# The second chunk's packed weights one step later, and the weight conversion as one stream through the second batch's attention

## The chip, the cores and the metric

The kernel runs on one core of a Trainium2 chip. The metric is device time in microseconds (us). Before the change the median of 3 runs is 812.47 us, from 811.91 to 814.41.

## The reference, cut to what matters

```
p_packed = sm_attn(p, k, v)             # 8 batches, 8 heads: 32 packed queries, 576 keys
out = sm_attn(q, p_packed, p_packed)    # 576 queries against the 32 packed rows
x = out.transpose(0, 2, 1, 3).reshape(B * S, H * D)     # 4608 tokens x 512
h = x @ w_in                            # 512 x 2048
g = h * tanh(softplus(h))               # "Mish"
return g @ w_out                        # 2048 x 512
```

Here `sm_attn(q, k, v)` is softmax(q k^T / 8) v. The two weight matrices come in as 64-bit floating-point numbers and are turned into 32-bit ones on the chip.

## The kernel before, in words

**Work per batch.** A batch's attention ends in a matrix `aT` (second softmax, transposed), held as a high and a low part, `aT_hi` and `aT_lo`. The values of the second attention are folded into `w_in`: `packed_w(b, c)` (L421) multiplies the packed rows of batch b with 512 columns of `w_in` (a *chunk* c, four of them) and splits the result into `wp_hi` (ScalarE, L439) and `wp_lo` (VectorE, L440). Then the work goes in *steps* t (`step`, L597), one for each pair of batch and 128 columns of `w_in`: `up` (L479) makes two halves of h with 6 matmuls each, ScalarE applies Mish (L482, L484), `halves` splits g into `g_hi` (ScalarE cast, L491, in the steps below 16) and `g_lo` (VectorE, L492), and two steps later `down` (L496 to L498) multiplies g with the matching 128 rows of `w_out` into four accumulators. So step t on TensorE is: a quarter of the down of step t-2, up half 0, two quarters of down, up half 1, the last quarter.

**Order of the steps.** `TURNS` lets batch 0 (`first`) do its columns 0 to 7 in steps 0 to 7, then batch 1 (`second`) all its 16 columns in steps 8 to 23, then batch 0 the rest. A chunk's packed weights are made at the end of the step named in L635: before the change, of every step with t % 4 == 2, so chunk 1 of batch 0, first read in step 4, is made at the end of step 2; chunk 0 of batch 1 at the end of step 6.

**Weight conversion.** Of each weight tile (`Weight` for 128 rows and 1024 columns of `w_in`, `WeightOut` for 128 rows of `w_out`) `fetch` issues a 512 KB load on the sync queue, `words` (L378, L379) is two ScalarE instructions, `join` (L383, L386, L387, L390) four VectorE instructions, and `done` either stores a pair of `w_in` tiles to DRAM (L395) or splits a `w_out` tile: `hi` is a ScalarE cast (L411) and `lo` a VectorE subtraction (L412). The list `weights` fixes their order: tiles 0 to 3 are the first half of `w_in`, tile 4 is `w_out` 0, then the second half's four tiles that chunk 1 needs (`w_in` chunk pair c = 1: tiles 5 to 8), then `w_out` 1 to 7 as tiles 9 to 15. The generator `conversion(n)` (L577) runs through them: an odd call does join(n), an even one words(n+1) and done(n). `take` calls it so many times; `step` takes half of its `n_conv` calls between the two up halves' places and the rest behind them.

**Who orders what.** TensorE's order is the order of the code throughout. Up to step 15 VectorE, ScalarE and the sync queue are in the order of the code too (`manual_schedule`); behind that a scheduler places them. Each engine works its list strictly in this order, so an instruction that waits holds up all that stands behind it.

**The start.** Lines L651 to L748 write out the attention of the first two batches by hand, with the conversions of tiles 0 to 5 between its pieces. `second.score_now(0)` (L706) is the first matmul of the second batch's keys; `exps_now` are its two exponentials on ScalarE; `first.weigh` finishes batch 0's second softmax on VectorE (L309 to L312), transposes it (L317), lets ScalarE cast it to `aT_hi` (L318) and subtracts to `aT_lo` (L319). `second.turn`, `turn_weights`, `values`, `turn_values` and `match` are batch 1's further pieces, `second.peak` and `second.weigh` its second softmax. Steps 0 and 1 stand between these pieces; steps 2 and on stand behind all of them, with 3 calls of the conversion in each of steps 2 to 7.

Of the kernel before, what the change touches and what calls it, by code (L numbers as in the profile page):

```python
# [8 lines left out]
F32 = mybir.dt.float32  # L9
# [26 lines left out]
def body(  # L36
# [101 lines left out]
    class Batch:  # L138
# [166 lines left out]
        def weigh(self, gs):  # L305
            a2 = self.a2[:, gs].rearrange("a h g n -> a (h g) n")
            G = a2.shape[1]
            sm = stat.tile([P, 2 * (S // NP)], F32, name="sm2")[:, :G]
            nc.vector.reduce_sum(out=sm, in_=a2, axis=AX.X)  # L309
            nc.vector.tensor_scalar(out=sm, in0=sm, scalar1=1e-9, scalar2=None, op0=ALU.add)  # L310
            nc.vector.reciprocal(out=sm, in_=sm)
            nc.vector.tensor_tensor(  # L312
                out=a2, in0=a2, in1=sm.unsqueeze(2).to_broadcast([P, G, NP]), op=ALU.mult
            )
            for g in range(gs.start, gs.stop):
                at = att.tile([P, S], F32, name="at", bufs=1)
                nc.vector.transpose(out=at, in_=self.a2[:, g].rearrange("a g n -> a (g n)"))  # L317
                nc.scalar.copy(out=self.aT_hi[:, g, :], in_=at)  # L318
                nc.vector.tensor_tensor(  # L319
                    out=self.aT_lo[:, g, :], in0=at, in1=self.aT_hi[:, g, :].bitcast(F32), op=ALU.subtract  # L320
                )

        def attention(self):


            self.start(ps_a)
            yield
            for g in range(2):
                yield from self.score(g, ps_a)
            self.exps(slice(0, 2))  # L330
            for g in range(2):
                yield from self.turn(g, ps_a)
            self.sums()
            for g in range(2):
                yield from self.turn_weights(g, ps_a)
                yield from self.values(g, ps_a)
            for g in range(2):
                yield from self.turn_values(g, ps_a)
            for g in range(2):
                yield from self.match(g, ps_a)  # L340
            self.peak(slice(0, 2))
            yield
            self.weigh(slice(0, 2))

    class Weight:

# [223 lines left out]
            paired[b // 2 * 2, f // 4] = t  # L570
    paired = {t: x for x, t in paired.items()}

    weights = [Weight(0, m) for m in range(4)] + [WeightOut(0)] + [Weight(1, m) for m in range(4)]
    weights += [WeightOut(i) for i in range(1, 8)] + [Weight(2, m) for m in range(4)] + [WeightOut(8)]
    weights += [Weight(3, m) for m in range(4)] + [WeightOut(i) for i in range(9, NF)]

    def conversion(n):  # L577
# [19 lines left out]
    def step(t, n_att, n_conv, cast):  # L597


        nonlocal gen  # L600
        grp = None
        if t < len(order):
            b, f, begin, end = order[t]
            if t == 20:
                gen = batches[2].attention()
            if b > 1 and f == 0 and b + 1 < B:
                gen = batches[b + 1].attention()
            if b > 1 and f == 10 and b + 2 < B:
                batches[b + 2].load()
            grp = Group(b, f, begin, end, wps[b, f // 4], g_rests[b // 2])  # L610
            grp.tiles()
        groups.append(grp)
        dn = groups[t - LAG] if t >= LAG else None
        if dn:
            down(dn, 0)
        if grp:
            grp.up(0)
        take(conv, n_conv // 2)
        take(gen, n_att[0])
        if dn:  # L620
            down(dn, 1)
            down(dn, 2)
        take(gen, n_att[1])
        if grp:
            grp.up(1)
        take(conv, n_conv - n_conv // 2)
        if grp:
            grp.halves(cast)
        if t - 1 in paired:
            pb, i = paired[t - 1]  # L630
            rest["g"] = split(g_rests[pb // 2][0, i], g_rests[pb // 2][1, i])
        if dn:
            down(dn, 3)
        n = t // 4 + 1
        if t % 4 == 2 and n < len(chunks):  # L635
            nb, nch = chunks[n]
            if nch == 0:
                together(gen)
            wps[nb, nch] = packed_w(nb, nch)
            if n >= 7 and n + 1 < len(chunks):  # L640
                fetch_wi(chunks[n + 1][1])
        else:
            take(gen, n_att[2])
        if t - 2 in paired:
            down_rest(*paired[t - 2])

    gen = iter(())
    with tc.manual_schedule(engines={mybir.EngineType.PE}):
# [4 lines left out]
        with tc.manual_schedule(engines={mybir.EngineType.DVE, mybir.EngineType.Activation, mybir.EngineType.SP}):  # L653
            for g in range(2):
                first.load_k(g)
                if g == 0:
                    first.load_p()
            w[0].fetch()
            for g in range(2):
                first.load_q(g)  # L660
            w[1].fetch()
            first.start(ps_a)
            first.turn_keys(0)
            first.score_now(0)
            w[0].words()
            sums = [first.exps_now(0)]
            first.turn_keys(1)
            for g in range(2):
                first.load_v(g)
            w[2].fetch()  # L670
            w[3].fetch()
            w[0].join()
            first.score_now(1)
            w[1].words()
            sums.append(first.exps_now(1))
            together(first.turn(0, ps_acc))
            w[1].join()
            w[1].done()
            first.sums_now(0, sums[0])
            together(first.turn_weights(0, ps_acc))  # L680
            together(first.turn(1, ps_acc))
            first.sums_now(1, sums[1])
            second.load_k(0)
            second.load_p()
            second.load_k(1)
            w[4].fetch()
            together(first.values(0, ps_a))
            together(first.turn_weights(1, ps_acc))
            w[2].words()
            w[2].join()  # L690
            together(first.values(1, ps_a))
            for g in range(2):
                together(first.turn_values(g, ps_a))
            w[3].words()
            for g in range(2):
                together(first.match(g, ps_acc))
            for g in range(2):
                second.load_q(g)
            w[5].fetch()
            for g in range(2):  # L700
                first.peak(slice(g, g + 1))
            second.start(ps_a)
            second.turn_keys(0)
            w[3].join()
            w[3].done()
            second.score_now(0)  # L706
            first.weigh(slice(0, 1))
            sums = [second.exps_now(0)]
            second.turn_keys(1)
            for g in range(2):  # L710
                second.load_v(g)
            for n in range(6, 11):
                w[n].fetch()
            wps = {(0, 0): packed_w(0, 0)}
            second.score_now(1)
            first.weigh(slice(1, 2))
            sums.append(second.exps_now(1))
            groups = []
            g_rests = [{} for _ in range(B // 2)]
            conv = iter(())  # L720
            together(second.turn(0, ps_acc))
            second.sums_now(0, sums[0])
            together(second.turn_weights(0, ps_acc))
            step(0, (0, 0, 0), 0, nc.scalar.copy)
            together(second.turn(1, ps_acc))
            second.sums_now(1, sums[1])
            w[4].words()
            w[4].join()
            together(second.values(0, ps_a))
            together(second.turn_weights(1, ps_acc))  # L730
            w[5].words()
            w[4].done()
            conv = conversion(5)
            together(second.values(1, ps_a))
            step(1, (0, 0, 0), 2, nc.scalar.copy)
            for g in range(2):
                together(second.turn_values(g, ps_a))
            for g in range(2):
                together(second.match(g, ps_acc))
            for g in range(2):  # L740
                second.peak(slice(g, g + 1))
            take(conv, 2)
            second.weigh(slice(0, 1))
            take(conv, 2)
            second.weigh(slice(1, 2))
            take(conv, 2)
            for t in range(2, START):
                step(t, (0, 0, 0), 3 if t < 8 or t == 11 else 1 if t == 10 else 2, nc.scalar.copy)  # L748
        for t in range(START, len(order) + LAG):
            if t in (16, 26):  # L750
                batches[t // 10 + 1].load()
# [27 lines left out]
```

## Time and profile before

| | |
|---|---|
| median of 3 runs | 812.47 us (811.91 to 814.41) |
| the profiled execution | 809.08 us |
| its span, first to last instruction | 807.3 us |
| TensorE matmul busy | 765.5 us, 95% of the span |
| VectorE busy | 441.9 us, 55% |
| ScalarE busy | 323.2 us, 40% |
| DMA mean rate | 106 GB/s |
| chain that ended last, by engine | PE 88%, DVE 9%, ACT 2% |

In the rows PE is TensorE's matmuls, PEld its weight loads, DVE is VectorE, ACT ScalarE, SPq the sync queue. A timeline row gives start, duration, engine, line, operation, the tile written and the tiles read, and in square brackets how long the engine sat idle before it and whose end released it. The durations of PE rows overlap, since matmuls are pipelined: the distance from one start to the next is the cost of one. PEclk is the share of full speed that TensorE's clock had.

### The profile page before, as it was taken

The page shows a single profiled execution, that of the slowest core. Times are in us where ns is not written, and L with a number is a line of the kernel's source. Part 1 is how long each engine was busy: PE and PEld are TensorE (multiplying, and loading weights), DVE is VectorE, ACT ScalarE, POOL GpSimd, SP SyncE. Part 2 cuts the span into 40 slices and gives each one's busy share as a digit, 9 for nine tenths or more (in the row PEclk, how much of TensorE's full clock was granted, in tenths as well). Part 3 has the DMA queues.
Part 4 walks back from the last instruction along what each step waited for, and adds up shares of the span by engine and source line. Part 5 has one row for each costly group of instructions (what it writes and reads, how often), then busy time and mean ns, then how long its engine had stood idle before and what let it go on. Part 6 is the DMA issues. An engine that isn't in the chain of part 4 may idle for free.

```text
span 807.3 us, 13715 instructions
## 1 busy us (share of the span) xinstructions
PE 765.5 (95%) x5584; PEld 608.5 (75%) x5584; DVE 441.9 (55%) x846; ACT 323.2 (40%) x752; POOL 0.7 (0%) x6
## 2 busy tenths in 40 slices
PE   7565799999999999999999999999999999999997
PEld 6344477887878787878788787888788787878886
DVE  4867887695457537354563546445473445532332
ACT  4353667563433424234342443334242343332221
POOL 0000000000000000000000000000000000000000
PEclk9667699999999999999999999999999999999999
DMA  9993205532522541242311532144311411131002
GB/s 251 302 293 113 104 27 157 161 127 79 172 90 79 158 141 59 76 138 92 111 53 59 176 96 76 56 154 125 112 53 53 137 40 54 53 105 53 1 1 65
DMA packets 42814, 85.82 MB, mean 106 GB/s; under 512 B 8448, under 2 KB 26880, under 8 KB 42752
## 3 DMA queue, kind: packets, MB, share of 16 engines
q1 hardware_dynamic: 42752, 84.95, 34.5%
q8 instruction: 44, 0.72, 0.4%
q14 instruction: 18, 0.15, 0.1%
HBM read 71.30 MB, written 13.63 MB: 105 GB/s over the span
## 4 chain that ended last, share of the span: by engine, by line
PE 88%; DVE 9%; ACT 2%; issue 1%; DMA 0%; SPq 0%; DVEq 0%; ACTq 0%
PE ps_h L479 25%; PE acc L496 15%; PE acc L498 14%; PE acc L497 14%; PE ps_w L428 4%; PE ps_kq L120 4%; PE ps_s L129 3%; PE ps_rest L496 2%; PE ps_rest L498 2%; PE ps_rest L497 2%; PE ps_pp L260 1%; PE ps_a L251 1%; DVE wi L387 1%; DVE wo L387 1%; DVE wo L390 1%
## 5 line engine op out<-in xcount | busy, mean ns | idle before, releaser
L496 PE MATMUL acc<-wo,g_hi 128*128 128x512 f32 x512 | 214.4, 419 | 1.9 <-ACT wo L411 1.1
L482 ACT ACTIVATE g<-ps_h 128x288 f32<-128x288 f32 (+1 forms) x256 | 98.2, 385 | 279.7 <-PE ps_h L479 229.2
L498 PE MATMUL acc<-wo,g_lo 128*128 128x512 f32 x512 | 202.6, 396 | 1.9 <-DVE g_lo L492 1.9
L497 PE MATMUL acc<-wo,g_hi 128*128 128x512 f32 x512 | 202.5, 395 | 0.0
L479 PE MATMUL ps_h<-aT_hi,wp_hi 128*128 128x288 f32 x512 | 157.6, 308 | 0.0
L491 DVE CAST g_hi<-g 128x512 fp32r<-128x512 f32 x112 | 47.8, 426 | 196.6 <-ACT g L482 196.6
L479 PE MATMUL ps_h<-aT_hi,wp_lo 128*128 128x288 f32 x512 | 152.8, 298 | 0.0
L479 PE MATMUL ps_h<-aT_lo,wp_hi 128*128 128x288 f32 x512 | 152.6, 298 | 0.0
L496 PEld LDWEIGHTS acc<-wo,g_hi 128*128 128x128 f32 x512 | 96.7, 189 | 45.1 <-issue 23.9
L498 PEld LDWEIGHTS acc<-wo,g_lo 128*128 128x128 f32 x512 | 96.8, 189 | 25.4 <-DVE g_lo L492 3.1
L479 PEld LDWEIGHTS ps_h<-aT_hi,wp_hi 128*128 128x128 f32 x512 | 97.6, 191 | 14.8 <-issue 5.6
L479 PEld LDWEIGHTS ps_h<-aT_lo,wp_hi 128*128 128x128 f32 x512 | 97.8, 191 | 8.8
L497 PEld LDWEIGHTS acc<-wo,g_hi 128*128 128x128 f32 x512 | 97.2, 190 | 8.6 <-DVE wo L412 0.4
L492 DVE TENSOR_TENSOR g_lo<-g,g_hi 128x512 fp32r<-128x512 f32 x128 | 88.2, 689 | 18.0 <-ACT g_hi L491 12.4
L479 PEld LDWEIGHTS ps_h<-aT_hi,wp_lo 128*128 128x128 f32 x512 | 97.7, 191 | 0.2 <-DVE wp_lo L440 0.2
L428 PE MATMUL ps_w<-wi,ppT 64*32 64x512 f32 x512 | 40.0, 628 | 13.7 <-DVE wi L390 10.1
L440 DVE TENSOR_TENSOR wp_lo<-ps_w,wp_hi 128x512 fp32r<-128x512 f32 x64 | 41.2, 682 | 19.1 <-ACT wp_hi L439 19.1
L439 ACT CAST wp_hi<-ps_w 128x512 fp32r<-128x512 f32 x64 | 34.4, 591 | 30.4 <-PE ps_w L428 30.4
L120 PEld LDWEIGHTS ps_kq<-ident,k_t 96*128 96x128 f32 x192 | 23.3, 162 | 6.8 <-issue 4.4
L484 ACT ACTIVATE g_rest<-ps_h 128x64 f32<-128x64 f32 x128 | 28.1, 219 | 0.0
L428 PEld LDWEIGHTS ps_w<-wi,ppT 64*32 64x32 f32 x512 | 6.4, 106 | 28.2 <-DVE wi L390 12.7
L120 PEld LDWEIGHTS ps_kq<-ident,q_t 96*128 96x128 f32 x192 | 21.9, 152 | 6.9 <-issue 3.0
(91 smaller groups left out, 753.4 us busy)
## 6 DMA issues: line engine op xcount, KB each, us to landing
wi<-w_in_f SPq DMA_DIRECT2D x48, 512.0 KB, 4.5
k_t<-in_k_dram SPq DMA_DIRECT2D x32, 288.0 KB, 3.6
q_t<-in_q_dram SPq DMA_DIRECT2D x32, 288.0 KB, 4.0
v_t<-in_v_dram SPq DMA_DIRECT2D x32, 288.0 KB, 3.9
w_st<-in_moe_w_in_dram SPq DMA_DIRECT2D x16, 512.0 KB, 6.4
w_st<-in_moe_w_out_dram SPq DMA_DIRECT2D x16, 512.0 KB, 4.4
out_dram<-o SPq DMA_DIRECT2D x24, 192.0 KB, 2.5
w_in_f<-wi SPq DMA_DIRECT2D x8, 512.0 KB, 4.8
```

The source lines that it names most:

```text
L120: nc.tensor.transpose(out=ps[:, h, :], in_=of_slot(src, g, h)[:, i, :], identity=ident[:R, :R])
L428: nc.tensor.matmul(out=ps[g][h * NP:(h + 1) * NP, :], lhsT=ppTb[row:row + D, g, h * NP:(h + 1) * NP], rhs=wis[c, g][row:row + D, h // 2, : ...
L439: nc.scalar.copy(out=hi, in_=ps[g])
L440: nc.vector.tensor_tensor(out=lo, in0=ps[g], in1=hi.bitcast(F32), op=ALU.subtract)
L479: nc.tensor.matmul(out=ps, lhsT=w[:, fs], rhs=a[:, g, cs], start=(n == 0), stop=(n == 5))
L482: nc.scalar.activation(out=self.act[:, hf * HALF:hf * HALF + m], in_=ps[:, :m], func=AF.Mish)
L484: nc.scalar.activation(out=self.g_rest[self.b % 2, self.f // 4][:, self.f % 4, :], in_=ps[:, m:], func=AF.Mish)
L491: cast(out=hi, in_=self.act)
L492: nc.vector.tensor_tensor(out=lo, in0=self.act, in1=hi.bitcast(F32), op=ALU.subtract)
L496: nc.tensor.matmul(out=acc, lhsT=hi[:, cs], rhs=wh, start=start, stop=False)
L497: nc.tensor.matmul(out=acc, lhsT=hi[:, cs], rhs=wl, start=False, stop=False)
L498: nc.tensor.matmul(out=acc, lhsT=lo[:, cs], rhs=wh, start=False, stop=stop)
```

## The change

Five edits, all in the part before step 16.

1. `weigh` is cut in three: `weigh` (the softmax's end), `back` (transpose and the ScalarE cast to `aT_hi`) and `low` (the subtraction to `aT_lo`), so that other work can stand between them.
2. `w_out` 1 becomes tile 5 of the list, ahead of the second half of `w_in`, whose four tiles become 6 to 9. `w_out` 2 to 7 stay tiles 10 to 15.
3. The conversion becomes one stream from tile 4 on: words(4) right behind `packed_w(0, 0)`, then a call or two behind nearly every piece of the second batch's attention and in steps 0 to 3. Steps 4 to 7 take 3, 2, 1 and 3 calls.
4. Chunk 1 of batch 0 is packed at the end of step 3 instead of step 2.
5. `first.weigh` moves behind the second batch's exponentials and key transposes; the second batch's scores for its second half stand ahead of `packed_w(0, 0)`; steps 2 and 3 now stand ahead of `second.weigh` of the first and of the second half.

```diff
@@ Batch.weigh
-            for g in range(gs.start, gs.stop):
-                at = att.tile([P, S], F32, name="at", bufs=1)
-                nc.vector.transpose(out=at, in_=self.a2[:, g].rearrange("a g n -> a (g n)"))
-                nc.scalar.copy(out=self.aT_hi[:, g, :], in_=at)
-                nc.vector.tensor_tensor(
-                    out=self.aT_lo[:, g, :], in0=at, in1=self.aT_hi[:, g, :].bitcast(F32), op=ALU.subtract
-                )
+        def back(self, g):
+            self.at = att.tile([P, S], F32, name="at", bufs=1)
+            nc.vector.transpose(out=self.at, in_=self.a2[:, g].rearrange("a g n -> a (g n)"))
+            nc.scalar.copy(out=self.aT_hi[:, g, :], in_=self.at)
+
+        def low(self, g):
+            nc.vector.tensor_tensor(
+                out=self.aT_lo[:, g, :], in0=self.at, in1=self.aT_hi[:, g, :].bitcast(F32), op=ALU.subtract
+            )
...
-    weights = [Weight(0, m) for m in range(4)] + [WeightOut(0)] + [Weight(1, m) for m in range(4)]
-    weights += [WeightOut(i) for i in range(1, 8)] + [Weight(2, m) for m in range(4)] + [WeightOut(8)]
+    weights = [Weight(0, m) for m in range(4)] + [WeightOut(0), WeightOut(1)]
+    weights += [Weight(1, m) for m in range(4)] + [WeightOut(i) for i in range(2, 8)]
+    weights += [Weight(2, m) for m in range(4)] + [WeightOut(8)]
...
-        if t % 4 == 2 and n < len(chunks):
+        if t % 4 == (2 if t > 3 else 3) and n < len(chunks):
...
             second.score_now(0)
-            first.weigh(slice(0, 1))
             sums = [second.exps_now(0)]
             second.turn_keys(1)
...
+            first.weigh(slice(0, 1))
+            first.back(0)
+            second.score_now(1)
+            first.low(0)
+            sums.append(second.exps_now(1))
+            first.weigh(slice(1, 2))
+            first.back(1)
             wps = {(0, 0): packed_w(0, 0)}
-            second.score_now(1)
-            first.weigh(slice(1, 2))
-            sums.append(second.exps_now(1))
+            w[4].words()
+            first.low(1)
...
-            conv = iter(())
+            conv = conversion(4)
             together(second.turn(0, ps_acc))
             second.sums_now(0, sums[0])
             together(second.turn_weights(0, ps_acc))
-            step(0, (0, 0, 0), 0, nc.scalar.copy)
+            take(conv, 1)
+            step(0, (0, 0, 0), 2, nc.scalar.copy)
             together(second.turn(1, ps_acc))
             second.sums_now(1, sums[1])
-            w[4].words()
-            w[4].join()
             together(second.values(0, ps_a))
             together(second.turn_weights(1, ps_acc))
-            w[5].words()
-            w[4].done()
-            conv = conversion(5)
+            take(conv, 2)
             together(second.values(1, ps_a))
             step(1, (0, 0, 0), 2, nc.scalar.copy)
...
             take(conv, 2)
+            step(2, (0, 0, 0), 2, nc.scalar.copy)
             second.weigh(slice(0, 1))
-            take(conv, 2)
+            second.back(0)
+            take(conv, 1)
+            second.low(0)
+            take(conv, 1)
+            step(3, (0, 0, 0), 2, nc.scalar.copy)
             second.weigh(slice(1, 2))
-            take(conv, 2)
-            for t in range(2, START):
-                step(t, (0, 0, 0), 3 if t < 8 or t == 11 else 1 if t == 10 else 2, nc.scalar.copy)
+            second.back(1)
+            take(conv, 1)
+            second.low(1)
+            take(conv, 1)
+            for t in range(4, START):
+                step(t, (0, 0, 0), {4: 3, 5: 2, 6: 1, 7: 3}.get(t, 2), nc.scalar.copy)
```

Three places in the built programs. Line numbers of the changed kernel from L323 on are 4 to 7 higher than before. First TensorE, at the end of step 2 before the change; `wo_91` is `w_out` 0, `wo_92` is `w_out` 1, `acc` an accumulator of down and `ps_w` the product of chunk 1 of batch 0:

```order
L496 MATMUL acc_874<-wo_91,g_hi 128x512
L497 MATMUL acc_874<-wo_91,g_hi 128x512
L498 MATMUL acc_874<-wo_91,g_lo 128x512
L428 MATMUL ps_w_924<-wi,ppT 32x512
L428 MATMUL ps_w_925<-wi,ppT 32x512
L428 MATMUL ps_w_924<-wi,ppT 32x512
L428 MATMUL ps_w_925<-wi,ppT 32x512
L428 MATMUL ps_w_924<-wi,ppT 32x512
L428 MATMUL ps_w_925<-wi,ppT 32x512
L428 MATMUL ps_w_924<-wi,ppT 32x512
L428 MATMUL ps_w_925<-wi,ppT 32x512
L496 MATMUL acc_871<-wo_92,g_hi 128x512
```

After the change the same product stands behind the last quarter of `wo_92` and ahead of `wo_93`, which is `w_out` 2:

```order
L503 MATMUL acc_854<-wo_92,g_hi 128x512
L504 MATMUL acc_854<-wo_92,g_hi 128x512
L505 MATMUL acc_854<-wo_92,g_lo 128x512
L435 MATMUL ps_w_959<-wi,ppT 32x512
L435 MATMUL ps_w_960<-wi,ppT 32x512
L435 MATMUL ps_w_959<-wi,ppT 32x512
L435 MATMUL ps_w_960<-wi,ppT 32x512
L435 MATMUL ps_w_959<-wi,ppT 32x512
L435 MATMUL ps_w_960<-wi,ppT 32x512
L435 MATMUL ps_w_959<-wi,ppT 32x512
L435 MATMUL ps_w_960<-wi,ppT 32x512
L503 MATMUL acc_851<-wo_93,g_hi 128x512
```

So all of step 3 has moved ahead of the packing of chunk 1. Second VectorE, behind the last subtraction of the second batch's `peak`; before, one `w_in` tile is joined here and `second.weigh` follows (`a_798` is the second batch's softmax):

```order
L300 TENSOR_TENSOR a_798<-a_798,mx_817 128x576
L383 TENSOR_SCALAR wi<-wi 128x512
L386 TENSOR_SCALAR wi<-wi 128x512
L387 SCALAR_TENSOR_TENSOR wi<-w_st,wi 128x512
L390 ISA wi<-wi,wround 128x1024
L309 TENSOR_REDUCE sm_832<-a_798 128x18
L310 TENSOR_SCALAR sm_832<-sm_832 128x18
L311 RECIPROCAL sm_832<-sm_832 128x18
L312 TENSOR_TENSOR a_798<-a_798,sm_832 128x576
L317 STREAM_TRANSPOSE at<-a_798 128x576
L319 TENSOR_TENSOR aT_lo<-at,aT_hi 128x576
```

After the change, at the same place (`a_816` is the same softmax):

```order
L300 TENSOR_TENSOR a_816<-a_816,mx_835 128x576
L390 TENSOR_SCALAR wi<-wi 128x512
L393 TENSOR_SCALAR wi<-wi 128x512
L394 SCALAR_TENSOR_TENSOR wi<-w_st,wi 128x512
L397 ISA wi<-wi,wround 128x1024
L390 TENSOR_SCALAR wi<-wi 128x512
L393 TENSOR_SCALAR wi<-wi 128x512
L394 SCALAR_TENSOR_TENSOR wi<-w_st,wi 128x512
L397 ISA wi<-wi,wround 128x1024
L499 TENSOR_TENSOR g_lo<-g,g_hi 128x512
L309 TENSOR_REDUCE sm_897<-a_816 128x18
```

Two joins and step 2's `g_lo` now come ahead of `second.weigh`. Before the change tiles 4 and 5 are joined above this place, after it tiles 4 to 7. Third ScalarE, around the cast to `aT_hi` of the second batch's second half; before (`wo_865` and `wo_907` are unsplit tiles of `w_out`):

```order
L318 CAST aT_hi<-at 128x576
L378 ACTIVATE wo_865<-w_st 128x512
L379 ACTIVATE wround<-w_st 128x512
L482 ACT_TABLE_LOAD
L482 ACTIVATE g<-ps_h 128x288
L482 ACTIVATE g<-ps_h 128x224
```

After the change (`ps_w_959` and `ps_w_960` are chunk 1's product, `wo_94` is `w_out` 3, and its unsplit tile is `wo_927`):

```order
L446 CAST wp_hi<-ps_w_959 128x512
L446 CAST wp_hi<-ps_w_960 128x512
L320 CAST aT_hi<-at 128x576
L385 ACTIVATE wo_985<-w_st 128x512
L386 ACTIVATE wround<-w_st 128x512
L418 CAST wo_94<-wo_927 128x512
L489 ACTIVATE g<-ps_h 128x288
L385 ACTIVATE wo_1009<-w_st 128x512
```

The cast now stands behind chunk 1's two casts, and the cast of `w_out` 3, for which VectorE's subtraction to `wo_94` waits, stands behind it and behind two conversion instructions.

More of the change, by code (lines that the diff above doesn't have):

```diff
@@ L343, in attention @@
             self.weigh(slice(0, 2))
+            for g in range(2):
+                self.back(g)
+                self.low(g)
     class Weight:
```

## The prediction

> **What bounds the kernel now.** I read first where TensorE loses time, with the busy times by stretch (start:end, length, then busy us of PE, PEld, DVE, ACT and POOL, PEclk, DMA share, GB/s):
>
> ```profile
> 35.07:66.38 31.31, 18.27 (x194) 13.02 (x192) 19.43 (x44) 16.05 (x37) 0.00 (x0) 0.64 0.88 265
> 66.38:107.28 40.90, 28.60 (x146) 19.82 (x147) 34.64 (x64) 21.97 (x43) 0.00 (x0) 0.75 0.26 90
> 118.77:806.00 687.23, 683.34 (x4902) 548.98 (x4902) 355.12 (x665) 262.18 (x623) 0.00 (x0) 1.00 0.30 94
> ```
>
> From 118.77 on TensorE is busy 683 of 687 us at full clock: whatever is won ahead of it arrives at the end undiminished, and nothing else can be won. Ahead of it TensorE waits. The table of waits for 35 to 119 us (total, times, longest) and TensorE's timeline say for whom:
>
> ```profile
> PE ps_w L428 <- DVE wi L390: 10.1, 2, 5.5
> PE acc L498 <- DVE g_lo L492: 1.9, 2, 1.3
> ...
> 74.21 1.04 PE L428 MATMUL ps_w<-wi,ppT 64*32 64x512 f32 x2
> ...
> 90.29 0.79 PE L496 MATMUL acc<-wo,g_hi 128*128 128x512 f32 x1 [1.08 <-ACT wo L411]
> ...
> 97.28 0.40 PE L496 MATMUL acc<-wo,g_hi 128*128 128x512 f32 x1
> ...
> 101.67 0.39 PE L496 MATMUL acc<-wo,g_hi 128*128 128x512 f32 x1
> ...
> 107.28 0.50 PE L498 MATMUL acc<-wo,g_lo 128*128 128x512 f32 x1 [0.60 <-DVE g_lo L492]
> ...
> 111.39 1.09 PE L428 MATMUL ps_w<-wi,ppT 64*32 64x512 f32 x16
> ...
> 118.77 0.50 PE L498 MATMUL acc<-wo,g_lo 128*128 128x512 f32 x1 [1.25 <-DVE g_lo L492]
> ```
>
> From 74.21 to 90.29 it stands in the packing of chunk 1, whose `w_in` tiles VectorE joins between the pieces of `second.weigh`. From 90.29 it runs: one step takes 101.67 - 97.28 = 4.39 us. It stops twice more, for VectorE's `g_lo` of step 4 (107.28, step 6) and of step 6 (118.77, step 8). So VectorE's list is the bound here, and I forecast by its rows: when does it reach `g_lo` of step 4 and of step 6?
>
> **The prices of VectorE's pieces.** One join, from its first instruction to the next piece's start, and the subtraction `lo` of a `w_out` tile with the wait for ScalarE's cast:
>
> ```profile
> 84.90 0.42 DVE L383 TENSOR_SCALAR wi<-wi 128x512 f32<-128x512 f32 x1
> ...
> 87.16 0.42 DVE L383 TENSOR_SCALAR wo<-wo 128x512 f32<-128x512 f32 x1
> ...
> 90.27 0.69 DVE L412 TENSOR_TENSOR wo<-wo,wo 128x512 fp32r<-128x512 f32 x1 [0.68 <-ACT wo L411]
> 90.88 0.42 DVE L383 TENSOR_SCALAR wo<-wo 128x512 f32<-128x512 f32 x1
> ```
>
> A join is 87.16 - 84.90 = 2.26 us, a `lo` 90.88 - 90.27 = 0.61, the bare wait for a cast 0.68. VectorE's own waits, from 35.07 to 66.38 (six rows) and from there to 107.28 (four):
>
> ```profile
> DVE g_lo L492 <- ACT g_hi L491: 5.6, 2, 3.4
> DVE wp_lo L440 <- ACT wp_hi L439: 2.4, 1, 2.4
> DVE aT_lo L319 <- ACT aT_hi L318: 1.5, 2, 0.7
> DVE mx L215 <- PE ps_s L129: 0.7, 1, 0.7
> DVE a1T L114 <- PE ps_a L251: 0.5, 1, 0.5
> DVE pp L268 <- PE ps_pp L260: 0.3, 1, 0.3
> ...
> DVE wo L412 <- ACT wo L411: 2.9, 4, 0.8
> DVE g_lo L492 <- ACT g_hi L491: 2.2, 1, 2.2
> DVE aT_lo L319 <- ACT aT_hi L318: 1.5, 2, 0.7
> DVE a L291 <- PE ps_s L129: 0.6, 1, 0.6
> ```
>
> The first table sums to 11.0. The 2.2 of the second is counted in the first already (it ends before 66.38); without it the second sums to 5.0.
>
> **Term 1, up to the copies of `ppT` (before: 66.38).** The change adds two joins here (tiles 6 and 7; tiles 4 and 5 are joined above this point in both) and one `lo` (`w_out` 1): 2 x 2.26 + 0.61 = 5.1 us. In return each of the six waits now has a join or a batch-0 piece in front of it: the 5.6 for `g_hi` and the 1.5 for `aT_hi` lie behind joins and behind the second batch's row maxima. What I find still bare in the new order: ScalarE's `aT_hi` and `wp_hi` casts ahead of `wp_lo` (two casts, 2 x 0.6 = 1.2), the cast of `w_out` 0 (0.7) and 0.2 of hand-overs, 2.1 in all. So 5.1 - (11.0 - 2.1) = -3.8: VectorE comes to `ppT` 3.8 us earlier with two joins more behind it. The DMA work of the moved tiles must have landed: below, as a rival.
>
> **Term 2, from `ppT` to `g_lo` of step 4 (before: 107.28).** Before, eight joins stand here (tiles 6 to 13), after, six (8 to 13), the `lo`s are four in both: -2 x 2.26 = -4.5 us. But the stream puts joins right behind their words. ScalarE's prices:
>
> ```profile
> 71.97 0.69 ACT L303 ACTIVATE a<-a 128x576 f32<-128x576 f32 x1 [0.77 <-DVE a L300]
> 72.56 0.66 ACT L378 ACTIVATE wi<-w_st 128x512 f32<-128x512 f32 x1
> ...
> 83.52 0.67 ACT L318 CAST aT_hi<-at 128x576 fp32r<-128x576 f32 x1 [4.73 <-DVE at L317]
> 84.10 0.66 ACT L378 ACTIVATE wo<-w_st 128x512 f32<-128x512 f32 x1
> 84.66 0.65 ACT L379 ACTIVATE wround<-w_st 128x512 int32<-128x512 uint32 x1
> 85.33 1.28 ACT L482 ACT_TABLE_LOAD   x1
> ...
> 89.62 0.62 ACT L411 CAST wo<-wo 128x512 fp32r<-128x512 f32 x1 [1.08 <-DVE wo L390]
> ...
> 93.72 0.41 ACT L482 ACTIVATE g<-ps_h 128x288 f32<-128x288 f32 x1 [1.98 <-PE ps_h L479]
> ```
>
> VectorE's waits in the new order: 0.6 for `match` as before; 1.3 ahead of join 8 (the last exponential, 0.59 to the next start, and the first of two word instructions, 0.66); 0.5 ahead of join 9 (words 8's second half 0.66, the table load 1.28, a Mish 0.41 and words 9's first half 0.66 take 3.0, against join 8 and its lead 2.5); 0.7 for the first `aT_hi`; three casts of `w_out` 2, 4 and 5, 0.7 each; and one long one. Behind the second `back` ScalarE casts `aT_hi` (0.58 to the next start), does words 12 (0.56 + 0.67) and only then casts `w_out` 3 (0.62), while VectorE's next instruction is that `lo`: 2.4 us bare, with words 13, join 12 and step 4's Mish queued behind on both engines. Sum 0.6 + 1.3 + 0.5 + 0.7 + 2.1 + 2.4 = 7.6 against 5.0. Term 2 is -4.5 + 2.6 = -1.9.
>
> So `g_lo` of step 4 comes 3.8 + 1.9 = 5.7 us earlier, at about 101.6. TensorE's moved packing costs nothing of that: by the same prices join 9 releases it near 75, `w_out` 2 near 83, `wp_lo` near 86 to 87; it waits there as it did before and then has 14 us for steps 4 and 5, 8.8 at full clock. Being some ten us ahead at step 4 buys it nothing at step 6.
>
> **Term 3, from step 6 to step 8.** Steps 5 and 6 hold 3 calls of the conversion instead of 6, so between the `g_lo` of step 4 and that of step 6 stand two joins instead of three and one `lo` instead of three: 101.6 + 2 x 2.26 + 0.68 + 0.61 + 2 x 0.69 = 108.8. TensorE asks for it at 101.6 + 2 x 4.39 + 1.09 (packing, the row at 111.39) = 111.5. The stop at 118.77 goes: -1.3 (its wait of 1.25 and a hand-over). One tile fewer is converted when step 16 starts; its `w_out` block (9) is read by step 19, so it is no term.
>
> **Sum.** 3.8 + 1.9 + 1.3 = 7.0 us. The profiled execution took 809.08 (span 807.3), the median of the runs is 812.47: I expect a span of 800.3, and 812.5 - 7.0 = 805.5 as the time. A measurement of this kernel tells about 0.3%, 2.4 us, from no change: faster means below 810.0.
>
> **Rivals.**
>
> *The clock falls in step 6 (0.25).* After step 5 TensorE waits some 2.3 us for ScalarE's cast of step 4, the last in its list behind words 14 and the cast of `w_out` 5. The trace shows what such a pause can do:
>
> ```profile
> 57.90:61.30 3.40, 1.27 (x51) 1.10 (x44) 3.01 (x7) 1.45 (x3) 0.00 (x0) 1.00 0.96 223
> 61.30:64.70 3.40, 2.75 (x13) 2.33 (x11) 2.16 (x5) 1.45 (x5) 0.00 (x0) 0.50 0.60 180
> ...
> 105.70:109.10 3.40, 2.80 (x15) 2.12 (x14) 3.21 (x7) 2.11 (x5) 0.00 (x0) 1.00 0.00 0
> ```
>
> A stretch with 1.27 of 3.4 us busy was followed by one at half clock; one with 2.80 busy was not. My 2.3 us pause leaves 1.1 to 2 busy. Half clock for 3.4 us costs 1.7: 805.5 + 1.7 = 807.2. The Trainium skill (page "TensorE: Matmul & The Clock Gate", section "HAM oscillation — how this bites in real kernels") asks only for no idle gap over about 3.4 us; by that the pause is harmless and the time stays 805.5. The trace disagrees: the gap inside the first row above is 3.40 - 1.27 = 2.1 us at most.
>
> *Term 1 doesn't come (0.16).* The stream puts four times two word instructions (1.2 us each pair) on ScalarE ahead of the casts, copies and Mish of the second batch's attention. For: VectorE's largest waits were for ScalarE. Against: ScalarE is busy 16.05 of 31.31 there. If they only move the waits, 3.8 goes: 7.0 - 3.8 = 3.2, 809.3; with the long wait of term 2 doubled as well (2.4), 811.7. That would be the change not doing what it says.
>
> *The words of `w_in`'s second half land late: slower (0.04).* Words 6 are now due near 53; before, ScalarE took that tile at 64.02.
>
> ```profile
> 39.41 1.30 SPq L371 DMA_DIRECT2D w_st<-in_moe_w_in_dram  x3
> ...
> 64.02 0.66 ACT L378 ACTIVATE wi<-w_st 128x512 f32<-128x512 f32 x1
> ...
> DMA to landing us min/median/max: 8.3/10.0/11.1
> ```
>
> Issued at 39.41 they land by 39.4 + 1.3 + 11.1 = 51.8 at the latest, 1 us ahead. If the queue (DMA share 0.88 there, and now eight instead of seven loads in this row) were 10 us later, ScalarE would stand in words 6 with the attention behind it: each us beyond 53 is a us lost, and beyond 53 + 7.0 + 2.4 = 62.4 the kernel is slower by over 0.3%; at 65 it would take 812.5 - 7.0 + 12 = 817.5.
>
> *More than forecast (0.05).* If the waits of 1.3 and 0.5 for words and one 0.7 are hidden, 2.5 more: 803.0.
>
> **How the numbers follow.** The forecast itself, 805.5, has 0.50. The range reaches from 803.0, less 0.5 for the medians' scatter (802.5), over the clock's 807.2 to the lower half of the rival without term 1, 810.0; outside lie about half of that rival, the late words and little else. Faster by over 0.3%: 0.50 + 0.25 + 0.05 + 0.05 of the third rival = 0.85, taken as 0.84; within 0.3%: 0.11; slower 0.05.
>
> **What would show it.** VectorE's first copy of `ppT` near 62.6, `g_lo` of step 4 near 101, TensorE's L505 of step 6 near 101.6, no wait at step 8. A 2.4 us wait of the `lo` of `w_out` 3 for its cast. TensorE still idle for some 6 us between 76 and 83, now ahead of `w_out` 2. The forecast is wrong if `ppT` comes later than 65, if ScalarE waits for the DMA of words 6, or if TensorE waits anew behind step 8.

## The result, and the profile after

| | before | after |
|---|---|---|
| median of 7 runs each, us | 812.61 (811.91 to 814.62) | 805.94 (804.13 to 810.02) |
| the profiled execution, us | 809.08 | 805.43 |
| its span, us | 807.3 | 803.6 |

The ratio of after to before over these runs is 0.9921, with a 95% interval of 0.9895 to 0.9946: the medians are 6.7 us apart, where 7.0 were forecast. The span of the profiled executions fell by 3.7 us only. The rows show why: busy times by stretch of the changed kernel (start:end, length, then PE, PEld, DVE, ACT, POOL, PEclk, DMA share, GB/s), cut at the same places as those of before, the first at the start of the second batch's softmax, the others at the copies of `ppT`, at `g_lo` of step 4 and in step 8.

```profile
36.88:64.75 27.87, 16.54 (x194) 11.58 (x192) 23.86 (x53) 18.32 (x40) 0.00 (x0) 0.71 0.97 298
64.75:103.26 38.51, 26.47 (x145) 19.49 (x145) 29.75 (x55) 19.06 (x38) 0.00 (x0) 0.82 0.23 82
103.26:115.16 11.90, 11.83 (x64) 9.11 (x65) 8.81 (x17) 7.73 (x20) 0.00 (x0) 0.86 0.00 0
115.16:802.20 687.04, 682.77 (x4905) 549.33 (x4903) 356.33 (x668) 263.28 (x625) 0.00 (x0) 1.00 0.30 94
```

From step 8 on nothing has changed: 683 of 687 us busy at full clock, as before. Everything lies ahead of that, and two things there hide part of the gain in the profiled execution.

First, the place at which the edited order begins comes later, though ahead of it only one load differs (by edit 2 it brings a `w_out` tile in place of a `w_in` tile). The instruction that I measure from is VectorE's `top` (L218) of the second batch's first half. The rows are before's, then after's; with it the two stretches ahead, 9 to 27 and 27 to 35 us:

```profile
9.00:27.00 18.00, 13.26 (x210) 8.90 (x210) 14.05 (x37) 10.19 (x24) 0.00 (x0) 1.00 1.08 296
27.00:35.00 8.00, 5.30 (x40) 4.12 (x41) 7.66 (x18) 2.12 (x4) 0.00 (x0) 0.51 1.09 270
...
35.00 0.15 DVE L218 TENSOR_SCALAR top<-top 128x1 f32<-128x1 f32 x1
```

```profile
9.00:27.00 18.00, 14.56 (x170) 11.09 (x178) 13.23 (x35) 9.95 (x24) 0.00 (x0) 0.50 1.08 310
27.00:35.00 8.00, 5.25 (x62) 2.98 (x46) 6.90 (x16) 2.12 (x4) 0.00 (x0) 0.50 1.08 261
...
36.88 0.15 DVE L218 TENSOR_SCALAR top<-top 128x1 f32<-128x1 f32 x1
```

Before's profiled execution had the full clock up to 27 us, after's half of it from the first row on, and `top` stands at 36.88 instead of 35.00. In the profiles of this study it stands between 35.0 and 39.5. Neither the clock nor the changed load is shown to be the cause: e1_pack_late_only, with the start of before and a clock of 0.99 from 9 to 27 us, has it at 37.33. So I read every profile from its own `top`:

| us behind `top` | before | after | forecast change | measured change |
|---|---|---|---|---|
| first copy of `ppT` | 31.38 | 27.87 | -3.8 | -3.5 |
| `g_lo` of step 4 on VectorE | 71.5 | 66.4 | -5.7 | -5.2 |
| first `g_lo` matmul of step 6 on TensorE | 72.3 | 67.1 | -5.7 | -5.2 |
| the same of step 8 | 83.77 | 78.74 | -7.0 | -5.0 |

Second, the clock falls in step 6. TensorE's timeline of after around steps 6 and 8, and three equal stretches around the drop:

```profile
103.19 0.50 PE L503 MATMUL acc<-wo,g_hi 128*128 128x512 f32 x1 [2.01 <-ACT g_hi L498]
...
104.00 0.78 PE L505 MATMUL acc<-wo,g_lo 128*128 128x512 f32 x1
...
115.16 0.39 PE L503 MATMUL acc<-wo,g_hi 128*128 128x512 f32 x1
115.39 0.40 PE L504 MATMUL acc<-wo,g_hi 128*128 128x512 f32 x1
115.62 0.40 PE L505 MATMUL acc<-wo,g_lo 128*128 128x512 f32 x1
```

```profile
101.00:104.40 3.40, 1.32 (x4) 0.70 (x4) 2.65 (x6) 2.40 (x7) 0.00 (x0) 0.95 0.01 2
104.40:107.80 3.40, 3.40 (x12) 2.98 (x12) 2.65 (x5) 2.00 (x4) 0.00 (x0) 0.55 0.00 0
107.80:111.20 3.40, 3.40 (x29) 2.03 (x29) 3.13 (x6) 1.37 (x4) 0.00 (x0) 1.00 0.00 0
```

The stop for `g_lo` at step 8 is gone: the three matmuls there stand 0.23 us apart. But the wait of 2.01 us for ScalarE's `g_hi` leaves 1.32 of 3.40 us busy, and the next 3.4 us run at half clock: 12 matmuls where the stretch behind it holds 29. That gives back about 3.4 / 2 = 1.7 us. The pause alone doesn't decide it, as e2_pack_early shows below.

VectorE's waits in after, from `top` to `ppT` and from there to `g_lo` of step 4:

```profile
DVE wp_lo L447 <- ACT wp_hi L446: 1.2, 1, 1.2
DVE wi L390 <- ACT wi L385: 1.0, 1, 1.0
DVE wo L419 <- ACT wo L418: 0.7, 1, 0.7
```

```profile
DVE wo L419 <- ACT wo L418: 4.4, 4, 2.4
DVE wi L390 <- ACT wi L385: 1.7, 2, 1.3
DVE aT_lo L323 <- ACT aT_hi L320: 0.7, 1, 0.7
DVE a L291 <- PE ps_s L129: 0.6, 1, 0.6
```

They sum to 2.9 (forecast 2.1) and 7.4 (forecast 7.6), the long one of 2.4 us among them. TensorE's waits in after from 60 to 125 us show the place of its longest stop, ahead of `w_out` 2, where 6 us were forecast:

```profile
PE acc L503 <- ACT wo L418: 5.9, 1, 5.9
```

### The profile page after: what moved, and what is told of

The parts are those of the page before. It is cut to its first block, busy times and chain, and to the rows that moved or that the text cites. A ratio compares the mean times of both kernels' runs of the same rounds, so it can differ in the third digit from the quotient of the medians.

```text
span 803.6 us, 13720 instructions
## 1 busy us (share of the span) xinstructions
PE 765.4 (95%) x5584; PEld 610.2 (76%) x5584; DVE 441.7 (55%) x846; ACT 322.7 (40%) x752; POOL 0.7 (0%) x6
## 4 chain that ended last, share of the span: by engine, by line
PE 86%; DVE 8%; ACT 2%; DMA 2%; issue 1%; SPq 0%; DVEq 0%; ACTq 0%
PE ps_h L486 24%; PE acc L503 15%; PE acc L505 14%; PE acc L504 14%; PE ps_kq L120 4%; PE ps_w L435 4%; PE ps_s L129 3%; PE ps_rest L503 2%; PE ps_rest L505 2%; PE ps_rest L504 2%; DMA w_st<-in_moe_w_out_dram 2%; PE ps_pp L260 2%; PE ps_a L251 1%; DVE wo L394 1%; DVE wo L397 1%
## 5 line engine op out<-in xcount | busy, mean ns | idle before, releaser
L435 PE MATMUL ps_w<-wi,ppT 64*32 64x512 f32 x512 | 36.2, 615 | 2.0 <-ACT a L223 2.0
L112 ACT COPY kT<-ps_kq 128x384 f32<-128x384 f32 x32 | 15.0, 480 | 28.4 <-PE ps_kq L120 28.4
```

Source lines behind the costliest of these rows:

```text
L435: nc.tensor.matmul(out=ps[g][h * NP:(h + 1) * NP, :], lhsT=ppTb[row:row + D, g, h * NP:(h + 1) * NP], rhs=wis[c, g][row:row + D, h // 2, : ...
```

## The experiments

The theory is the prediction's: VectorE's list sets the time, the pieces of the stream fill its waits up to `ppT` (3.8 us), and fewer joins stand behind `ppT` (1.9). The rivals: the later packing is the gain, because TensorE's wait of 10.1 us for joined `w_in` tiles goes; or the new order of the front is the gain, and the stream is not needed for it. For every run the table gives the mark of step 8 (the first `g_lo` matmul, us behind `top`, from its one profile) beside the ratio to the kernel before. Runs sharing a comparison share its runs of before (medians 812.3 of 28 runs for the first four, 813.66 of 15 for the last four). The two groups ran on two chips, so kernels of different groups are compared by their ratios.

| kernel | step 8 | median us | ratio to before (95%) |
|---|---|---|---|
| before | +83.8 | | 1 |
| after | +78.7 | 805.94 | 0.9921 (0.9895 to 0.9946) |
| e1_pack_late_only | +88.7 | 816.45 | 1.0047 (1.0029 to 1.0066) |
| e2_pack_early | +79.3 | 808.37 | 0.9952 (0.9933 to 0.9971) |
| e3_old_front | +84.7 | 812.16 | 0.9989 (0.9970 to 1.0008) |
| e4_front_only | +78.2 | 805.68 | 0.9911 (0.9887 to 0.9935) |
| e5_exps_first | +81.0 | 809.63 | 0.9955 (0.9936 to 0.9974) |
| e6_calls_ahead | +73.2 | 802.03 | 0.9852 (0.9825 to 0.9879) |
| e7_keep_warm | +77.9 | 805.19 | 0.9894 (0.9864 to 0.9924) |
| e8_words_ahead | +69.7 | 797.93 | 0.9808 (0.9781 to 0.9835) |

### The later packing alone: e1_pack_late_only

The kernel before, with edit 4 alone.

```diff
-        if t % 4 == 2 and n < len(chunks):
+        if t % 4 == (2 if t > 3 else 3) and n < len(chunks):
```

> The kernel before with only edit 4: chunk 1 of batch 0 is packed at the end of step 3. Theory (VectorE's list is the bound): TensorE no longer stands in the packing, but in the down of step 3, whose first row block needs w_out 1, cast at 89.6 us of the profile before; step 3 starts at 90.3 as before. The packing (1.1) and wp_lo now come after it, so step 4 starts some 2.7 us later, and the stops at steps 6 and 8, which are set by VectorE, take most of that up: 812.6 + 0.4 to 2, 813 to 815 us. Rival (the gain of the change is the 10.1 us wait in the packing, removed by packing a step later): 806 to 807 us.

It is slower by 0.5%, 3.8 us, and more so than expected. TensorE's waits from 60 to 125 us, then VectorE's from 70:

```profile
PE acc L496 <- ACT wo L411: 15.9, 1, 15.9
```

```profile
DVE wo L412 <- ACT wo L411: 8.8, 6, 4.1
```

The same row of before:

```profile
DVE wo L412 <- ACT wo L411: 4.2, 6, 0.8
```

The wait for the joined tiles went and one of 15.9 us for a `w_out` tile came in its place: TensorE was early for something else. And VectorE now waits 8.8 us for casts of `w_out`, where in before it waits 4.2 in six casts over the same stretch; `g_lo` of step 4 comes 4.9 us later (76.48 against 71.54 behind `top`). Removing TensorE's wait is no gain by itself.

### After with the early packing: e2_pack_early

```diff
-        if t % 4 == (2 if t > 3 else 3) and n < len(chunks):
+        if t % 4 == 2 and n < len(chunks):
```

> The changed kernel without edit 4: chunk 1 of batch 0 is packed at the end of step 2 again. Theory: VectorE's list up to g_lo of step 4 holds the same pieces; wp_lo comes ahead of the second weigh and waits there 1.2 us for ScalarE's casts, which are then bare. Step 6 starts about 1.2 us later: 805.9 + 1.2 = 807.1, 806 to 808 us. Rival (packing a step later makes the gain): back by most of the 6.7 us, 811 to 813 us.

Against before it gains 0.48% where after gains 0.79%: some 2.4 us of after's gain need edit 4, twice the 1.2 expected. The intervals of the two ratios overlap a little (from 0.9933 to 0.9946), so the sign is likely, the size rough. Its profile agrees in part: `g_lo` of step 4 comes 2.1 us later than in after, with a wait of 2.0 for `wp_hi` that after has not.

```profile
DVE wp_lo L447 <- ACT wp_hi L446: 2.0, 1, 2.0
```

At step 8 only 0.6 of the 2.1 are left in this execution, since it kept its full clock in step 6: from step 6 to step 8 it takes 10.1 us, where after takes 11.6. Yet TensorE's pause ahead of step 6 is the same as in after, 2.00 us to its 2.01:

```profile
106.37 0.50 PE L503 MATMUL acc<-wo,g_hi 128*128 128x512 f32 x1 [2.00 <-ACT g_hi L498]
```

From 104.10 to 107.50 TensorE is busy 1.32 of 3.40 us here too, and the clock of the next 3.4 us is 1.00. So the same pause was followed by half clock in after and not in e2_pack_early; what decides is open.

With the stream the later packing helps; without it (e1) it harms.

### After without the new front: e3_old_front

The order of edit 5 at the start is taken back; stream, tile list and later packing stay.

```diff
+            first.weigh(slice(0, 1))
+            first.back(0)
+            first.low(0)
             sums = [second.exps_now(0)]
...
-            first.weigh(slice(0, 1))
-            first.back(0)
-            second.score_now(1)
-            first.low(0)
-            sums.append(second.exps_now(1))
-            first.weigh(slice(1, 2))
-            first.back(1)
             wps = {(0, 0): packed_w(0, 0)}
+            second.score_now(1)
+            first.weigh(slice(1, 2))
+            first.back(1)
+            first.low(1)
+            sums.append(second.exps_now(1))
             w[4].words()
-            first.low(1)
```

> The changed kernel with the old order of the first batch's weigh, the second batch's scores and packed_w(0, 0), while the stream, the tile list and the later packing stay. From VectorE's top of the second batch's first half to its first copy of qT the profile before has 14.9 us and the profile after 11.1. Theory: these 3.8 us come back and nothing behind them takes them up, since VectorE's list stays the bound up to step 6: 805.9 + 3.8 = 809.7, 809 to 811 us. Rival (the stream alone makes the gain, the front is hidden behind ScalarE and TensorE): 806 us.

The whole gain is gone, more than the 3.8 us expected: 0.9989, an interval that holds 1. VectorE's waits from `top` to the copies of `ppT`:

```profile
DVE wp_lo L447 <- ACT wp_hi L446: 2.4, 1, 2.4
DVE aT_lo L323 <- ACT aT_hi L320: 1.5, 2, 0.7
DVE wo L419 <- ACT wo L418: 1.5, 1, 1.5
DVE wi L390 <- ACT wi L385: 1.0, 1, 1.0
DVE mx L215 <- PE ps_s L129: 0.7, 1, 0.7
DVE a1T L114 <- PE ps_a L251: 0.5, 1, 0.5
```

The 2.4, 1.5 and 0.7 of before are back, although the stream is there. It cannot stand in their place: they lie ahead of its first join. The first copy of `ppT` stands at +33.09, 5.2 us behind after's: the 3.8 lost up to `qT` (+14.94), 0.8 more of the wait for the cast of `w_out` 0 (1.5 for 0.7), whose words now follow the late exponentials on ScalarE, and the 0.5 for `ps_a`.

### The new front alone: e4_front_only

The kernel before with the front of after and nothing else: the old tile list, the old conversions, the early packing.

```diff
             second.score_now(0)
-            first.weigh(slice(0, 1))
             sums = [second.exps_now(0)]
...
+            first.weigh(slice(0, 1))
+            first.back(0)
+            second.score_now(1)
+            first.low(0)
+            sums.append(second.exps_now(1))
+            first.weigh(slice(1, 2))
+            first.back(1)
             wps = {(0, 0): packed_w(0, 0)}
-            second.score_now(1)
-            first.weigh(slice(1, 2))
-            sums.append(second.exps_now(1))
+            first.low(1)
             w[4].words()
```

> The kernel before with only the new order of the front (first weigh, scores and packed_w(0, 0) as in the changed kernel), with the old tile list, the old places of the conversion and the packing at the end of step 2. Theory: VectorE comes 3.8 us earlier to the first copy of qT, all that follows waits for the same things as before and moves with it: 812.6 - 3.8 = 808.8, 808 to 810 us. Rival (the stream alone makes the gain): 812 to 813 us.

It is as fast as the whole change: 0.9911 against 0.9921. I had expected a little over half of it. It wins 3.8 us up to the second batch's first copy of `qT` (14.94 to 11.12 behind `top`), the very 3.8 that after wins there, and another 2.4 up to `ppT` (31.38 to 25.21). ScalarE shows where that comes from. Its waits, from 35 us to about the copies of `ppT`, in before and in e4_front_only:

```profile
ACT aT_hi L318 <- DVE at L317: 11.5, 2, 5.8
```

```profile
ACT aT_hi L320 <- DVE at L319: 3.7, 2, 2.3
```

Before, ScalarE stood 5.8 us twice in front of a cast to `aT_hi`, waiting for VectorE's softmax and transpose, with the second batch's exponentials behind it. These need VectorE's `top`, and in e4_front_only they start 0.25 us behind its start. So they were ready only for the later half of each wait, some 2.7 us. The rows of before's second wait, `top` and the cast:

```profile
45.60 0.15 DVE L218 TENSOR_SCALAR top<-top 128x1 f32<-128x1 f32 x1
...
48.56 0.67 ACT L318 CAST aT_hi<-at 128x576 fp32r<-128x576 f32 x1 [5.79 <-DVE at L317]
```

In the new front the exponentials run in that time, and all of ScalarE's later work is there sooner. VectorE's waits up to `ppT` in e4_front_only, against the 11.0 us of before:

```profile
DVE g_lo L499 <- ACT g_hi L498: 3.7, 2, 2.6
DVE wp_lo L447 <- ACT wp_hi L446: 1.2, 1, 1.2
DVE pp L268 <- PE ps_pp L260: 0.4, 1, 0.4
```

That is 5.3, so 5.7 fewer with no join moved. What the stream, the list and the later packing add up to: e4_front_only is 2.7 ahead of after at `ppT` (25.21 against 27.87), 0.4 ahead at `g_lo` of step 4 and 0.5 at step 8, where after's profiled execution lost 1.7 by the clock. As built they are worth nothing that these runs resolve.

### The exponentials first: e5_exps_first

The kernel before, in which only ScalarE's order changes: each `exps_now` stands ahead of `first.weigh`.

```diff
-            first.weigh(slice(0, 1))
             sums = [second.exps_now(0)]
+            first.weigh(slice(0, 1))
...
-            first.weigh(slice(1, 2))
             sums.append(second.exps_now(1))
+            first.weigh(slice(1, 2))
```

> The kernel before with two lines moved: the exponentials of the second batch's keys (exps_now, ScalarE) come ahead of each first.weigh. VectorE's order and TensorE's order stay as before. Theory, formed after the new order of the front alone had given the whole gain: before, the exponentials stand in ScalarE's list behind the cast to aT_hi, which waits for VectorE (11.5 us of ScalarE's waits from 35 to 67 us), and hold up packed_w(0, 0), the copies of qT and step 0. Most of the front's 6.6 us come with this alone: 806 to 808 us, first copy of qT 11.5 to 12.5 us after VectorE's top. Rival (VectorE's own new order makes the gain): 811 to 813 us.

It wins 0.45% (3.7 us) of the front's 0.89%, 2.4 of the 3.8 us up to `qT` (14.94 to 12.54 behind `top`) and 2.8 of the 5.6 at step 8: about half of the gain is ScalarE's order alone. I had expected most of it: 809.63 lies between my range and the rival's. TensorE shows the way by which it comes. Before, its packing of chunk 0 stood behind these exponentials:

```profile
39.18 2.44 PE L428 MATMUL ps_w<-wi,ppT 64*32 64x512 f32 x16 [3.57 <-ACT a L223]
```

In e5_exps_first that wait is 0.29 us and VectorE's 2.4 us wait for `wp_hi` is gone. By subtraction the rest belongs to VectorE's and TensorE's order (scores ahead of the packing, `weigh` behind the key copies); no run takes these two apart.

### The conversion calls ahead of the softmax: e6_calls_ahead

After's 2.4 us wait stands behind ScalarE's cast to `aT_hi`. After's ScalarE, then its VectorE, at that place:

```profile
92.37 0.67 ACT L320 CAST aT_hi<-at 128x576 fp32r<-128x576 f32 x1 [5.71 <-DVE at L319]
92.95 0.68 ACT L385 ACTIVATE wo<-w_st 128x512 f32<-128x512 f32 x1
93.54 0.65 ACT L386 ACTIVATE wround<-w_st 128x512 int32<-128x512 uint32 x1
94.09 0.61 ACT L418 CAST wo<-wo 128x512 fp32r<-128x512 f32 x1
```

```profile
91.56 0.78 DVE L319 STREAM_TRANSPOSE at<-a 128x576 f32<-128x576 f32 x1
94.73 0.69 DVE L419 TENSOR_TENSOR wo<-wo,wo 128x512 fp32r<-128x512 f32 x1 [2.39 <-ACT wo L418]
```

ScalarE waits 5.71 us, and then does in one piece what VectorE wants at once. The edit moves one call ahead of each `second.weigh`, and the join that follows between transpose and `low`:

```diff
+            take(conv, 1)
             second.weigh(slice(0, 1))
             second.back(0)
             take(conv, 1)
             second.low(0)
-            take(conv, 1)
             step(3, (0, 0, 0), 2, nc.scalar.copy)
+            take(conv, 1)
             second.weigh(slice(1, 2))
             second.back(1)
             take(conv, 1)
             second.low(1)
-            take(conv, 1)
```

> The changed kernel with one conversion call moved ahead of each second.weigh, so that a join stands between back and low and the cast of w_out 3 no longer stands behind the second cast to aT_hi. Theory (the stream wins nothing because its own waits on VectorE, 7.4 us from ppT to g_lo of step 4, eat the two joins it saves there): the waits of 2.4, and 0.7 for aT_hi, twice in effect, go; g_lo of step 4 comes 3.1 us earlier and the time is 805.9 - 3.1 = 802.8, 801.5 to 804.5 us. Rival (TensorE's steps 4 and 5, partly at half clock, bound step 6 by now): 805 to 806 us.

As expected and a little better: 0.9852, and `g_lo` of step 4 stands 4.0 us earlier than in after (62.4 behind `top`), with `ppT` where it was. VectorE's waits from `ppT` to that `g_lo`:

```profile
DVE wi L390 <- ACT wi L385: 1.7, 2, 1.3
DVE a L291 <- PE ps_s L129: 1.1, 1, 1.1
DVE wo L419 <- ACT wo L418: 0.7, 1, 0.7
```

The casts of `w_out` fell from 4.4 to 0.7, the wait for `aT_hi` is gone, and the sum fell from 7.4 to 3.5: the whole 4.0 us within 0.1. TensorE's wait for `g_hi` ahead of step 6 fell from 2.01 to 1.30 us, and this execution kept its full clock there.

### TensorE kept busy behind step 5: e7_keep_warm

After, with 12 matmuls behind step 5 that nothing reads.

```diff
+                if t == 5:
+                    fill = ps_a.tile([P, FC], F32, name="ps_fill", tag="ps_a")
+                    for _ in range(12):
+                        nc.tensor.matmul(
+                            out=fill[:, :HALF], lhsT=wps[0, 1][0][0][:, :P], rhs=first.aT_hi[:, 0, :HALF],
+                            start=True, stop=True,
+                        )
```

> The changed kernel with 12 matmuls of 288 columns more on TensorE behind step 5, where it waits 2.0 us for ScalarE's cast; their result is read by nobody. Theory (the pause lets the clock fall in step 6, as the profile after shows for 3.4 us): no stretch at half clock between steps 5 and 8, step 8 starts 77.0 to 77.5 us after VectorE's top instead of 78.7, and the time is about 805.9 - 1.7 = 804.2 us. Rival (a pause under 3.4 us leaves the clock alone and the stretch came from something else): the stretch stays, 806 us or a little more.

Three stretches around the place where after lost its clock:

```profile
100.00:103.40 3.40, 2.36 (x14) 1.76 (x13) 2.61 (x6) 1.72 (x5) 0.00 (x0) 1.00 0.02 5
103.40:106.80 3.40, 2.97 (x19) 2.60 (x19) 2.65 (x5) 1.89 (x5) 0.00 (x0) 1.00 0.01 2
106.80:110.20 3.40, 3.32 (x18) 2.60 (x17) 2.61 (x6) 2.11 (x6) 0.00 (x0) 1.00 0.00 0
```

No stretch falls to half clock, and from step 6 to step 8 it takes 77.9 - 67.8 = 10.1 us instead of after's 78.7 - 67.1 = 11.6: that is 1.5 of the 1.7. Step 8 stands at +77.9, 0.8 earlier than in after and not the 1.2 to 1.7 expected, for step 6 itself came 0.7 later. The ratio, 0.9894 with an interval of 0.9864 to 0.9924, cannot be told from after's: the price of the drop is shown in the profile, not in the time. Nor is it shown that the 12 matmuls kept the clock: e2_pack_early kept it without them and takes the same 10.1 us from step 6 to step 8.

### The words of three tiles one place earlier: e8_words_ahead

e6_calls_ahead, and besides one call more ahead of `values(1)`, one behind step 1, and one fewer in each of steps 1 and 2, so that tiles 7, 8 and 9 have their words earlier than VectorE reaches their joins.

```diff
-            take(conv, 2)
+            take(conv, 3)
             together(second.values(1, ps_a))
-            step(1, (0, 0, 0), 2, nc.scalar.copy)
+            step(1, (0, 0, 0), 1, nc.scalar.copy)
+            take(conv, 1)
...
-            step(2, (0, 0, 0), 2, nc.scalar.copy)
+            step(2, (0, 0, 0), 1, nc.scalar.copy)
```

> As the run with the calls ahead of the weighs, and also the words of tiles 7, 8 and 9 one place earlier on ScalarE, where it stood idle, so that VectorE's joins 7, 8 and 9 needn't wait for them (1.0, 1.3 and 0.4 us in the profile after). Theory (VectorE's list is the bound): g_lo of step 4 comes 3.1 + 2.7 = 5.8 us earlier than in the changed kernel, 800.1 us; TensorE comes near its own bound there, so 799.5 to 802 us. Rival (TensorE's steps 4 and 5 are the bound by now): no better than 803 us.

0.9808, better than expected and the lowest of all; before (1) and after (0.9921) lie outside its interval. `g_lo` of step 4 is 7.5 us ahead of after's, `ppT` 1.0. VectorE's waits from `ppT` to that `g_lo`:

```profile
DVE wo L419 <- ACT wo L418: 0.7, 1, 0.7
DVE a L291 <- PE ps_s L129: 0.6, 1, 0.6
```

Of 7.4 us there 1.3 are left; that is 6.1 of the 7.5, and 1.0 was won ahead of `ppT`. So the stream isn't worthless: it wins 83.8 - 69.7 = 14.1 us at step 8 together with the front, where the front alone wins 5.6. As the change built it, its own waits ate what it saved.

## Why the prediction was right, and where its reasons were not

**What bounds the kernel.** Right, and borne out by the runs: the marks of VectorE's list set the time. Read from `top`, step 8 puts the ten kernels in the order of their ratios, but for before and e3_old_front, whose marks lie 0.9 us apart and whose times are the same. Removing TensorE's own wait (e1) won nothing.

**Term 1, up to `ppT` (-3.8).** It measured -3.5, and its parts nearly so: VectorE's busy time there grew by 23.86 - 19.43 = 4.4 (5.1 forecast), its waits fell from 11.0 to 2.9 (2.1 forecast; the 1.0 for the words of tile 7 was not seen coming). The size is right, the reason half wrong. "In return each of the six waits now has a join or a batch-0 piece in front of it" lumped two edits. Three of the six rows (2.4 for `wp_hi`, 1.5 for `aT_hi`, 0.7 for `ps_s`) lie ahead of the copy of `qT`, where no join stands in either kernel. What removes 3.4 of their 4.6 us is edit 5 alone (e4), and the largest row, the 2.4 for `wp_hi`, goes already when only the second batch's exponentials no longer queue behind a cast that waits (e5). The two joins then filled what was left of the waits for `g_hi`, at a net loss of 2.7 us up to `ppT` against the front alone. I never priced the edits apart.

**Term 2, from `ppT` to `g_lo` of step 4 (-1.9).** Measured: 66.4 - 27.87 against 71.5 - 31.38, so -1.6. The waits came as listed, 7.4 against 7.6, with the 2.4 us wait for the cast of `w_out` 3 at the place named. e6 and e8 showed what such waits cost: 3.9 and 6.1 us of them taken out brought `g_lo` of step 4 forward by 4.0 and, with `ppT` 1.0 earlier, by 7.5.

**Term 3, the stop at step 8 (-1.3).** The stop is gone as forecast. Without the clock's drop the distance from step 6 to step 8 is 10.1 us (e2, e7), against before's 11.5: -1.4. In after's profiled execution the drop undoes it (11.6).

**The moved packing.** It "costs nothing of that": right in after. That it helps there, by some 2 us (e2), and harms without the stream (e1), was not seen.

**The rivals.** The clock's drop in step 6 did come in the profiled execution, with the pause (2.01 us against the 2.3 forecast) and the size (1.7) as worked out. The Trainium skill (page "TensorE: Matmul & The Clock Gate", section "HAM oscillation — how this bites in real kernels") would have let this pause pass, as it is shorter than about 3.4 us. The half clock that followed in after speaks against that as a sufficient rule; in e2_pack_early the same pause did pass. The median fell by 6.7 us: the mark at step 8 accounts for 5.0 of them, behind it the span is 0.5 shorter (803.6 - 115.62 against 807.3 - 118.77), and the last us is smaller than the scatter of the runs, 2.7 to 5.9 us from lowest to highest. That 6.7 lies so near to the 7.0 forecast is in part luck: in the profiled executions only 5.0 of the 7.0 stand at step 8. ScalarE did not wait for the DMA of the words of tile 6, and term 1 did come. (The moved `w_in` tiles hold 512 columns each, as the joins' rows of 128x512 show, and are the quarter of `w_in` for chunk 1, not a half; no price hangs on that. The 0.05 put down to the third rival under "How the numbers follow" is more than its 0.04; it fits only the rival without term 1.)

**What stays open.** Why the clock at the start of some executions is halved from 9 us on and of others only from 27, and why the pause ahead of step 6 is followed by half clock in after and not in e2_pack_early.

## What to carry to other kernels

In a list that an engine works in order, look first for an instruction that waits long with ready work behind it: here ScalarE's cast stood 5.8 us twice, the next exponentials ready behind it for the later half, and moving two lines won about half of what the front is worth. When work is moved into waits, price the new order with and without each edit, since two edits that fill the same wait don't add. Put the producer's half of a split task (here the words and the cast) a place ahead of the consumer's long piece: two calls moved so took the ratio from 0.9921 to 0.9852.

## What the runs showed of the hardware that was not expected

- Half the clock over the 18 us from 9 to 27 us isn't shown to delay what follows. At 0.50 there, `top` came at 36.88 (after) and 39.00 (e6_calls_ahead); at 0.99 to 1.00 it came at 35.00 (before), 37.33 (e1_pack_late_only) and 37.94 (e2_pack_early). The DMA share there is 1.07 or 1.08 in all five. Before and e1_pack_late_only have the same instructions ahead of it, and so have the other three, so it scatters by some us from one execution to the next.
- A pause of 2.0 us, well inside a stretch of 3.4 us, can be followed by 3.4 us of half clock, and the same pause need not be: 1.32 of 3.40 us busy was followed by it in after and not in e2_pack_early. A shorter pause is no surety either: in e1_pack_late_only half clock follows from about 105 us on, and TensorE's longest wait in the 12 us ahead of it is 1.03 us (at 103.13).
